# A looped TensorE stream, and a new path for x, in a one-token attention kernel that streams 554 MB

## The chip, the cores and the metric

The kernel runs on one core of one Trainium2 chip. The metric is the device time of one execution in microseconds (us).

Words used below: TensorE multiplies matrices, VectorE and ScalarE work on elements, SyncE's queue issues the large loads ("the main queue"), and ScalarE's queue is "the second queue". Each of the large loads is spread over 16 DMA engines (it leaves 16 completion records); it has landed when the last of the 16 has reported (in the kernel before, the 16 records of K31 came from 1230.87 to 1237.35 us, and the product that waits for it started at 1237.44 us). P.V is the product of the softmax weights with V. "K31" and "V31" are K and V of the last of the 32 heads, which are counted from 0. Engines get their instructions by DMA too: the profile lists these transfers as queues of kind "instruction" (q8 and q14). q8 carries TensorE's: 33 packets before. Such a transfer is called a fetch, and the 16 KB of one packet of q8 a block.

## The reference, cut to what matters

```python
# x: [1, 1, 640]   K, V caches: [1, 32 heads, 32768, 128]   all bf16
xn = layernorm(x)
q = (xn @ wq)                       # 32 heads of 128
p = softmax(q . k_cache * 128**-0.5)    # one query against 32768 keys, per head
out = x + (p . v_cache) @ wo + (silu(xn @ w_gate) * (xn @ w_up)) @ w_down
```

Each head needs 8.39 MB of K and 8.39 MB of V. With the weights that makes 554 MB, each byte read once.

## The kernel before

Three slots of 8.39 MB form a ring. The main queue loads wq, the feed-forward weights, then K0, K1, V0, K2, V1 and so on, at the end wo and the last V in five pieces. A load may start when its slot has been used up.

```python
@block.sync
def sp(e):
    e.dma_start(xb[:, :], A_x[0, 0:1, :].rearrange("o (p c) -> (o p) c", c=NCD)).then_inc(s_x, 16)  # 128 rows of 10 bytes
    for u in units:
        s = slot_of[u]
        if s in owner:
            e.wait_ge(*owner.pop(s))         # scores done (K slot) or P.V done (V slot)
        ...                                  # the load
```

VectorE multiplies K by the query in four pieces, TensorE sums each piece over groups of the head dimension with the identity as weights (`scores`), VectorE finishes the sums and the maximum, ScalarE takes the exponential. P.V of one head runs beside the next head's scores. TensorE's stream is one long straight line, written out for all 32 heads:

```python
@block.tensor
def pe(t):
    ...
    for k in range(NK):                      # 32 heads, written out
        scores(k)                            # 4 x 16 matmuls on the identity, 128x512 each
        ...
        total(h - 1)
        halves = pv_ops(h - 1, c); next(halves)   # 32 weight loads and 32 matmuls
        turn(h)                              # maximum over partitions
        next(halves)                         # 32 more
        spread(h)
        fold(h - 2)
    fold(H - 2)
    ...
    for h in range(H - 1): att(h)            # 155 one-column matmuls with wo
    total(H - 1)
    pv(H - 1, 0)                             # last head: 256 one-column matmuls, in five pieces as V lands
    att(H - 1)
```

Every wait is on a constant, for example `t.wait_ge(s_mul, n + 1)`.

## Time and profile before

| | before |
|---|---|
| time, median of 3 runs | 1299.28 us (1298.93 to 1299.52) |
| span of the profile | 1297.3 us |
| busy share: TensorE / VectorE / ScalarE | 80% / 52% / 4% |
| read from memory over the span | 427 GB/s |

From the page of the kernel before: the line of 40 slices (each digit is the busy share of the 16 DMA engines in tenths), the queue table (packets, MB, share of the 16 engines' span), and one group of TensorE's instructions (count, busy time and mean; then the idle time ahead of them and what ended most of it).

```profile
DMA  9999999999999999999999999999999999999997
...
q1 hardware_dynamic: 14848, 554.00, 99.2%
q8 instruction: 33, 0.54, 0.2%
q14 instruction: 6, 0.05, 0.0%
...
L245 PE MATMUL ps<-ring,ident 128*128 128x512 bf16 x128 | 56.2, 439 | 228.8 <-DVE ring L485 228.6
```

The DMA engines work from end to end: q1's packets alone take 99.2% of the 16 engines' span. The line L245 is the first score matmul of each piece: TensorE waits 228.6 us in all for VectorE there, so it is not what sets the pace. The queue's own timeline (start, duration, instruction) shows that it has a reserve too:

```profile
870.01 0.33 SPq L185 DMA_DIRECT2D ring<-in_A_v_cache_dram  x1
```

The load ahead of the one issued at 870.01 us lands on its fastest DMA engine at about 882 us, so the engines have 12 us of work left when a new load joins.

The same trace holds one record per DMA packet, and each transfer leaves 16 completion records. From them I computed, for eight loads, how far the last of the 16 lies behind the first. This is a computed table, not a view of the profile:

```
kernel before: time since wq's first packet (us) and spread of the 16 completions (us)
 load at    28   183   338   493   648   802   957  1112
 spread    1.2   1.9   1.9   3.4   3.4   4.9   4.9   6.4
```

The fastest engine takes 19.35 us per 8.39 MB load from first to last (8.39 MB / 19.35 us = 433.5 GB/s if all 16 went so), but others fall behind in steps of 1.5 us. The queue q8 suggests the reason: 33 instruction packets of 16,384 bytes, about one per head, 1.07 us each on average. The page counts 5142 matmuls and 3222 weight loads of TensorE, so a packet brings about 253 of its instructions (8364 / 33), and one instruction takes about 65 bytes. Every eight of them the spread grows by 1.5 us. At K31's landing seven of the 16 engines are within 1.6 us of the first, one is 4.3 us behind it, and eight are 4.8 to 6.5 us behind.

If all 16 engines kept the pace of the fastest, the load at 1112 us would land up to 6.4 us earlier (an estimate from the table). So the gain was sought with the slower engines; whether the fastest could go faster was not shown.

The end of the span, from the view by windows (us from the start; busy time of each engine, granted clock of TensorE, share of the DMA engines at work, GB/s):

```profile
core 0: us, PE busy (x) PEld busy (x) DVE busy (x) ACT busy (x) POOL busy (x), PEclk, DMA share, GB/s
...
1285.00:1288.00 3.00, 2.50 (x94) 2.41 (x91) 0.00 (x0) 0.00 (x0) 0.00 (x0) 0.50 0.58 236
1288.00:1290.00 2.00, 0.00 (x0) 0.00 (x0) 0.00 (x0) 0.00 (x0) 0.00 (x0) 0.50 0.44 172
```

Between 1285 and 1290 us only about half of the DMA engines still work: this is the spread again. And the timeline of the end (start, duration, engine, line, operation, count, idle time before and its releaser):

```profile
1237.44 17.43 DVE L485 TENSOR_TENSOR ring<-ring,qb 128x8192 bf16<-128x8192 bf16 x4 [2.85 <-DMA ring<-in_A_k_cache_dram]
...
1276.26 6.33 PE L340 MATMUL ps<-ocol,ring 128*128 128x1 bf16 x155 [0.36 <-ACT ocol L397]
...
1282.88 4.62 PE L270 MATMUL ps<-P,ring 128*128 128x1 bf16 x160
...
1290.12 2.72 PE L270 MATMUL ps<-P,ring 128*128 128x1 bf16 x96 [2.62 <-issue]
1292.87 0.22 DVE L514 TENSOR_SCALAR ocol<-ps,rzb 128x1 bf16<-128x1 f32 x1 [9.65 <-PE ps L270]
```

L485 is VectorE's product for the last head's K (K31), L340 the output product of heads 0 to 30, L270 the last head's P.V. There is a gap of 2.62 us in L270 after 160 of 256 columns, put down to "issue": a wait for nothing that the profile shows. (The last piece of V landed at 1290.41 us by its semaphore's records, the second piece, which holds columns 128 to 191, at 1285.51 us.) The start, for comparison with the change:

```profile
0.74 0.38 SPq L164 DMA_DIRECT2D xb<-in_A_x_dram  x1
...
1.18 0.41 SPq L171 DMA_DIRECT2D ring<-in_A_wq_dram  x1
...
52.42 8.76 DVE L485 TENSOR_TENSOR ring<-ring,qb 128x8192 bf16<-128x8192 bf16 x2 [6.30 <-DMA ring<-in_A_k_cache_dram]
```

### The profile page before, as it was taken

The numbers are of one execution on the slowest core, as the hardware profiler recorded it, in microseconds if no ns is written. First come the engines' busy times: TensorE is split into PE (matmuls) and PEld (weight loads), VectorE is DVE, ScalarE is ACT, GpSimd is POOL, SyncE is SP. The second block draws the span as 40 slices with busy tenths as digits, with TensorE's granted clock in tenths as the row PEclk, the third lists the DMA queues.
The fourth block names the chain that finished last, engine by engine and source line by source line (L and its number), as shares of the span: only waits on it lengthen the run. The fifth ranks groups of instructions, "written<-read, shape, count | busy, mean of one in ns | idle before, by whom it ended". The sixth has DMA issues, their size and how long they took to land.

```text
span 1297.3 us, 9428 instructions
## 1 busy us (share of the span) xinstructions
PE 1036.7 (80%) x5142; PEld 263.8 (20%) x3222; DVE 669.7 (52%) x406; ACT 50.8 (4%) x139; POOL 1.1 (0%) x8
## 2 busy tenths in 40 slices
PE   3678879877779877778877779877778978778977
PEld 1301222111222111222111222111222111222115
DVE  0485444666444666444666444666444566444560
ACT  2000000000000000000000000000000000000000
POOL 0000000000000000000000000000000000000000
PEclk9589889888889888889888889888889888889886
DMA  9999999999999999999999999999999999999997
GB/s 399 435 434 425 441 431 435 428 435 431 441 425 433 433 436 431 427 439 427 447 421 435 435 427 445 421 443 426 435 435 427 443 423 439 429 438 429 433 395 288
DMA packets 14887, 554.59 MB, mean 427 GB/s; under 512 B 1472, under 2 KB 5632, under 8 KB 5888
## 3 DMA queue, kind: packets, MB, share of 16 engines
q1 hardware_dynamic: 14848, 554.00, 99.2%
q8 instruction: 33, 0.54, 0.2%
q14 instruction: 6, 0.05, 0.0%
HBM read 553.99 MB, written 0.00 MB: 427 GB/s over the span
## 4 chain that ended last, share of the span: by engine, by line
DMA 52%; PE 30%; DVE 15%; issue 3%; SPq 0%; ACT 0%; DVEq 0%
DMA ring<-in_A_k_cache_dram 52%; PE ps L274 17%; DVE ring L485 14%; PE ps L228 10%; PE ps L245 1%; PE ps L270 1%; PE ps L340 1%; PE ps L310 0%; PE ps L304 0%; PE ps L295 0%; SPq L190 0%; DVE sc L493 0%; PE ps L316 0%; ACT o L392 0%; SPq L192 0%
## 5 line engine op out<-in xcount | busy, mean ns | idle before, releaser
L485 DVE TENSOR_TENSOR ring<-ring,qb 128x8192 bf16<-128x8192 bf16 x128 | 557.8, 4419 | 91.6 <-DMA ring<-in_A_k_cache_dram 91.6
L228 PE MATMUL ps<-ring,ident 128*128 128x512 bf16 x1920 | 495.3, 416 | 0.0
L274 PE MATMUL ps<-ring,P 128*4 128x512 bf16 x1984 | 438.3, 379 | 0.0
L245 PE MATMUL ps<-ring,ident 128*128 128x512 bf16 x128 | 56.2, 439 | 228.8 <-DVE ring L485 228.6
L274 PEld LDWEIGHTS ps<-ring,P 128*4 128x4 bf16 x1984 | 166.1, 85 | 245.3
L245 PEld LDWEIGHTS ps<-ring,ident 128*128 128x128 bf16 x128 | 12.6, 98 | 624.6 <-DVE ring L485 534.8
L508 DVE TENSOR_SCALAR negb<-ps 128x1 f32<-128x1 f32 x32 | 5.1, 158 | 215.5 <-PE ps L316 215.5
L493 DVE TENSOR_REDUCE sc<-ps 128x64 f32<-128x512 f32 x128 | 82.2, 683 | 62.1 <-PE ps L228 62.1
L503 DVE TENSOR_REDUCE m<-ps 1x1 f32<-1x128 f32 x32 | 8.9, 279 | 192.3 <-PE ps L310 192.3
L409 ACT ACTIVATE P<-sc,negb 128x256 bf16<-128x256 f32 x32 | 16.2, 508 | 1187.4 <-DVE negb L508 1187.4
L295 PE MATMUL ps<-identf,o 4*128 4x1 f32 x248 | 31.9, 245 | 0.9 <-ACT o L392 0.9
L304 PEld LDWEIGHTS ps<-rsum,ones 128*128 128x128 f32 x64 | 12.3, 194 | 99.2 <-issue 98.4
L295 PEld LDWEIGHTS ps<-identf,o 4*128 4x128 f32 x248 | 30.0, 187 | 0.9 <-ACT o L392 0.9
L392 ACT ACTIVATE o<-ps,rzb 4x512 f32<-4x512 f32 x31 | 21.0, 677 | 0.0
L220 PE MATMUL ps<-ring 128*128 128x512 bf16 x40 | 10.7, 436 | 11.7 <-DMA ring<-in_A_wq_dram 11.7
L454 DVE TENSOR_SCALAR sg<-sg 128x13 f32<-128x13 f32 (+1 forms) x2 | 0.2, 154 | 34.9 <-ACT sg L385 34.9
L500 DVE TENSOR_REDUCE pmax<-sc 128x1 f32<-128x256 f32 x32 | 13.4, 420 | 0.0
L310 PE MATMUL ps<-identf,pmax 128*1 128x128 f32 x64 | 12.2, 273 | 1.2 <-DVE pmax L500 1.2
L325 PE MATMUL ps<-xn,ring 128*128 128x1 bf16 (+1 forms) x140 | 8.7, 198 | 5.3 <-DMA ring<-in_B_w_down_dram 5.3
L316 PE MATMUL ps<-m,ones 1*128 1x1 f32 x64 | 12.1, 256 | 0.4 <-DVE m L503 0.4
L316 PEld LDWEIGHTS ps<-m,ones 1*128 1x128 f32 x64 | 9.4, 183 | 14.2 <-issue 13.5
L473 DVE RECIPROCAL rzb<-ps 128x1 f32<-128x1 f32 x32 | 5.0, 157 | 9.8 <-PE ps L304 9.8
(47 smaller groups left out, 87.8 us busy)
## 6 DMA issues: line engine op xcount, KB each, us to landing
ring<-in_A_wq_dram SPq DMA_DIRECT2D x1, 5120.0 KB, 15.3
ring<-in_A_wo_dram SPq DMA_DIRECT2D x1, 5120.0 KB, 36.7
ring<-in_A_v_cache_dram SPq DMA_DIRECT2D x1, 4096.0 KB, 22.0
ring<-in_B_w_gate_dram SPq DMA_DIRECT2D x1, 2160.0 KB, 20.0
ring<-in_B_w_up_dram SPq DMA_DIRECT2D x1, 2160.0 KB, 24.6
ring<-in_B_w_down_dram SPq DMA_DIRECT2D x1, 2080.0 KB, 28.6
ring<-in_A_v_cache_dram SPq DMA_DIRECT2D x1, 2048.0 KB, 21.4
ring<-in_A_v_cache_dram SPq DMA_DIRECT2D x1, 1024.0 KB, 23.3
```

Of the source, the lines that this page charges most:

```text
L228: return t.add_instruction(mybir.InstMatmult(start_tensor_calc=False, stop_tensor_calc=stop, tile_size=(128, 128), tile_position=(0, 0), l ...
L245: t.matmul(ob, lhsT=ident[:, :], rhs=src, start=True, stop=False)
L270: mm = t.matmul(OL, lhsT=ring[:, s, j * DH:(j + 1) * DH], rhs=P[:, h % PR, jj:jj + 1], start=(jj == 0), stop=(jj == NJ - 1))
L274: mm = t.matmul(O[h % 2], lhsT=P[:, h % PR, jj:jj + W], rhs=ring[:, s, j * DH:(j + W) * DH], start=(jj == 0), stop=(jj + W == NJ))
L295: mm = t.matmul(fold_ps, lhsT=o4[:, m * DH:(m + 1) * DH], rhs=identf[0:W, m:m + 1], start=(m == 0), stop=(m == W - 1))
L316: t.matmul(misc[:, 128:129], lhsT=ones[0:1, :], rhs=m1[0:1, h % SR:h % SR + 1], start=True, stop=True).then_inc(s_b, 1)
L340: mm = t.matmul(acc[:, c:c + 1], lhsT=wo_v[:, h, :, c], rhs=ocol[:, h:h + 1], start=(h == 0 and c == 0), stop=(h == H - 1), skip_group_che ...
L392: a.activation(out=o4[:, :], in_=O[h % 2], func=ACTF.Copy, scale=rzb[0:W, h % SR:h % SR + 1]).then_inc(s_o4, 1)
L409: a.activation(out=P[:, h % PR, :], in_=sc[:, h % SCR, :], func=ACTF.Exp, bias=negb[:, h % SR:h % SR + 1], scale=c_scale, accum_out=rsum[: ...
L485: v.tensor_tensor(out=kh, in0=kh, in1=q[:, None, :].to_broadcast([128, HF, DH]), op=ALU.mult).then_inc(s_mul, 1)
L493: v.tensor_reduce(out=sc[:, h % SCR, j:j + HF], in_=bank[n % NBK].rearrange("p (j e) -> p j e", e=G), axis=AX.X, op=ALU.add).then_inc(s_re ...
L500: v.tensor_reduce(out=pmax[:, h % SR:h % SR + 1], in_=sc[:, h % SCR, :], axis=AX.X, op=ALU.max).then_inc(s_max, 1)
```

## The change

There are two parts. TensorE's heads 2 to 31 become a loop of ten passes over three heads, so that TensorE's built program has 466 + 446 + 426 instructions (ahead of the loop, in it, behind it) in place of 5142, the separate weight loads not counted; what a wait counts to is then computed into a register. And x comes as one row on the second queue and is turned into a column by five small matmuls, so that wq is the first load of the main queue. To make three heads a period, the statistics slots go from 4 to 3 and the output bank from two to one; the wait for the feed-forward result moves ahead of the first head.

```diff
-    SR = 4
+    H0, PER = 2, 3
+    SR = 3
...
-            O = [ps8[0:W, 4, :], ps8[0:W, 5, :]]
+            O = ps8[0:W, 4, :]
...
             def sp(e):
-                e.dma_start(xb[:, :], A_x[0, 0:1, :].rearrange("o (p c) -> (o p) c", c=NCD)).then_inc(s_x, 16)
...
             def pe(t):
+                t.wait_ge(s_x, 16)
...
+                for c in range(NCD):
+                    mm = t.matmul(misc[:, 8 + c:9 + c], lhsT=xrow_v[:, :, c], rhs=one1[:, :], start=True, stop=True)
...
+                def wait(sem_of, h, count):
+                    n = count(h)
+                    if group[0] is not None:
+                        d = count(h + PER) - n
...
+                        n = group[0] * d + n          # a register
+                    t.wait_ge(sem_of, n)
...
-                for k in range(NK):
-                    scores(k)
-                    ...
+                for h in range(H0):
+                    head(h)
+                with t.Fori(0, (H - H0) // PER) as i:
+                    group[0] = i
+                    for h in range(H0, H0 + PER):
+                        head(h)
...
             def act(a):
+                a.dma_start(xrow, A_x[0, 0:1, :]).then_inc(s_x, 16)
```

More of the change, by code (lines that the diff above doesn't have):

```diff
@@ L33, in bass_parallel_sum__gqa_block_cached__swiglu_ffn__decode_kernel @@
     NJ = SK // 128
-    CH = NJ
-    NCH = NJ // CH
     HF = 64
-    NHF = CH // HF
-    NSTEP = NCH * NHF
+    NHF = NJ // HF
     G = 512 // HF
-    assert NJ % CH == 0 and CH % HF == 0 and DH % G == 0
-    CE = CH * DH
-    NK = H * NCH
+    assert NJ % HF == 0 and DH % G == 0
+    CE = NJ * DH
     FB = (F + 127) // 128
@@ L47, in bass_parallel_sum__gqa_block_cached__swiglu_ffn__decode_kernel @@
     SLOTS = 3
-    NBK = 4
-    SCR = 1
+    H0, PER = 2, 3
     PR = 3
-    SR = 4
+    SR = 3
     TAIL = [128, 64, 32, 16, 16]
     W = 512 // DH
-    assert sum(TAIL) == CH
+    assert sum(TAIL) == NJ and NHF == 4 and (H - H0) % PER == 0 and PER % SLOTS == 0
+    assert PER % PR == 0 and PER % SR == 0
     c_scale = float(DH) ** -0.5
@@ L60, in bass_parallel_sum__gqa_block_cached__swiglu_ffn__decode_kernel @@
     for h in range(H):
-        for c in range(NCH):
-            units.append(("k", h, c))
-            if h >= 1:
-                units.append(("v", h - 1, c))
-    units += [("wo",)]
-    units += [("v", H - 1, c) for c in range(NCH)]
+        units.append(("k", h))
+        if h >= 1:
+            units.append(("v", h - 1))
+    units += [("wo",), ("v", H - 1)]
     slot_of, use_of = {}, {}
@@ L75, in bass_parallel_sum__gqa_block_cached__swiglu_ffn__decode_kernel @@
     WQ_S, FFN_S, WO_S = slot_of[("wq",)], slot_of[("ffn",)], slot_of[("wo",)]
-    LASTV = ("v", H - 1, NCH - 1)
+    LASTV = ("v", H - 1)
     with ExitStack() as es:
@@ L86, in bass_parallel_sum__gqa_block_cached__swiglu_ffn__decode_kernel @@
         qb = sbt("qb", [128, H * DH], BF16)
-        sc = sbt("sc", [128, SCR, NJ], F32)
+        sc = sbt("sc", [128, NJ], F32)
         P = sbt("P", [128, PR, NJ], BF16)
@@ L95, in bass_parallel_sum__gqa_block_cached__swiglu_ffn__decode_kernel @@
         sg = sbt("sg", [128, 2, FB], F32)
-        xb = sbt("xb", [128, NCD], BF16)
+        one1 = sbt("one1", [1, 1], BF16)
         xf = sbt("xf", [128, NCD], F32)
@@ L129, in bass_parallel_sum__gqa_block_cached__swiglu_ffn__decode_kernel @@
         x0 = WQ_S * CE + NCD * H * DH
+        xrow = flat[0:1, x0 + NCD * 128:x0 + NCD * 128 + D]
+        xrow_v = xrow.rearrange("o (m c) -> o m c", c=NCD)
         xnb = flat[:, x0:x0 + NCD * 128].rearrange("p (c m) -> p c m", c=NCD)
-        assert NCD * (H * DH + 128) <= CE
+        assert NCD * (H * DH + 256) <= CE
         wq_v = wq.rearrange("p (c n) -> p c n", c=NCD)
@@ L155, in bass_parallel_sum__gqa_block_cached__swiglu_ffn__decode_kernel @@
             bank = [ps8[:, b, :] for b in range(8)]
-            O = [ps8[0:W, 4, :], ps8[0:W, 5, :]]
-            OL = ps8[:, 4 + (H - 1) % 2, 0:1]
+            O = ps8[0:W, 4, :]
+            OL = ps8[:, 5, 0:1]
             acc = ps8[:, 6, 0:NCD]
@@ L173, in sp @@
                     elif u[0] == "k":
-                        _, h, c = u
-                        e.dma_start(ring[:, s, :], kv_src(A_k_cache, h, c * CH, CH)).then_inc(s_slot[s], 16)
-                        owner[s] = (s_qk, NHF * (h * NCH + c + 1))
+                        e.dma_start(ring[:, s, :], kv_src(A_k_cache, u[1], 0, NJ)).then_inc(s_slot[s], 16)
+                        owner[s] = (s_qk, NHF * (u[1] + 1))
                     elif u == LASTV:
@@ L180, in sp @@
                             e.dma_start(ring[:, s, j * DH:(j + n) * DH],
-                                        kv_src(A_v_cache, H - 1, NJ - CH + j, n)).then_inc(s_tail[i], 16)
+                                        kv_src(A_v_cache, u[1], j, n)).then_inc(s_tail[i], 16)
                             j += n
                     elif u[0] == "v":
-                        _, h, c = u
-                        e.dma_start(ring[:, s, :], kv_src(A_v_cache, h, c * CH, CH)).then_inc(s_slot[s], 16)
-                        owner[s] = (s_pv, h * NCH + c + 1)
+                        e.dma_start(ring[:, s, :], kv_src(A_v_cache, u[1], 0, NJ)).then_inc(s_slot[s], 16)
+                        owner[s] = (s_pv, u[1] + 1)
                     elif u[0] == "ffn":
@@ L209, in pe @@
             def pe(t):
-                t.wait_ge(s_a, 3)
+                t.wait_ge(s_x, 16)
+                t.wait_ge(s_a, 2)
+                for c in range(NCD):
+                    mm = t.matmul(misc[:, 8 + c:9 + c], lhsT=xrow_v[:, :, c], rhs=one1[:, :], start=True, stop=True)
+                mm.then_inc(s_pa, 1)
+                t.wait_ge(s_a, 4)
                 t.matmul(misc[:, 0:1], lhsT=ones[:, :], rhs=st[:, 0:1], start=True, stop=True).then_inc(s_pa, 1)
-                t.wait_ge(s_a, 6)
+                t.wait_ge(s_a, 7)
                 t.matmul(misc[:, 1:2], lhsT=ones[:, :], rhs=st[:, 2:3], start=True, stop=True).then_inc(s_pa, 1)
-                t.wait_ge(s_a, 10)
+                t.wait_ge(s_a, 11)
                 t.wait_ge(s_wq, 16)
@@ L231, in again, with scores @@
                         ins=[nc.tensor.lower_ap(rhs), nc.tensor.lower_ap(lhsT)], outs=[nc.tensor.lower_ap(out)]))
-                def scores(k):
-                    h, c = divmod(k, NCH)
-                    kv = ring[:, slot_of[("k", h, c)], :].rearrange("p (j d) -> p j d", d=DH)
-                    for i in range(NHF):
-                        n = k * NHF + i
-                        t.wait_ge(s_mul, n + 1)
-                        if n >= NBK:
-                            t.wait_ge(s_red, n - NBK + 1)
-                        ob = bank[n % NBK].rearrange("p (j e) -> p j e", e=G)
+                group = [None]
+                def wait(sem_of, h, count):
+                    n = count(h)
+                    if group[0] is not None:
+                        d = count(h + PER) - n
+                        assert all(count(h + PER * i) == n + d * i for i in range((H - H0) // PER))
+                        n = group[0] * d + n
+                    t.wait_ge(sem_of, n)
+                def scores(h):
+                    kv = ring[:, slot_of[("k", h)], :].rearrange("p (j d) -> p j d", d=DH)
+                    for i in range(NHF):
+                        wait(s_mul, h, lambda h: NHF * h + i + 1)
+                        if h >= 1:
+                            wait(s_red, h, lambda h: NHF * (h - 1) + i + 1)
+                        ob = bank[i].rearrange("p (j e) -> p j e", e=G)
                         for g in range(DH // G):
@@ L248, in scores @@
                         mm.then_inc(s_qk, 1)
-                def pv_ops(h, c):
-                    u = ("v", h, c)
-                    s = slot_of[u]
-                    if c == 0:
-                        t.wait_ge(s_exp, h + 1)
-                        if h >= 2:
-                            t.wait_ge(s_o4, h - 1)
-                    parts = [(None, CH)]
-                    if u == LASTV:
-                        parts = list(enumerate(TAIL))
-                    j = 0
-                    for i, n in parts:
-                        if i is None:
-                            t.wait_ge(s_slot[s], 16 * use_of[u])
-                        else:
-                            t.wait_ge(s_tail[i], 16)
-                        end = j + n
-                        while j < end:
-                            jj = c * CH + j
-                            if h == H - 1:
-                                mm = t.matmul(OL, lhsT=ring[:, s, j * DH:(j + 1) * DH],
-                                              rhs=P[:, h % PR, jj:jj + 1], start=(jj == 0), stop=(jj == NJ - 1))
-                                j += 1
-                            else:
-                                mm = t.matmul(O[h % 2], lhsT=P[:, h % PR, jj:jj + W],
-                                              rhs=ring[:, s, j * DH:(j + W) * DH], start=(jj == 0),
-                                              stop=(jj + W == NJ))
-                                j += W
-                            if j == CH // 2:
-                                yield
@@ new lines, in pv_half @@
+                def pv_half(h, half):
+                    s = slot_of[("v", h)]
+                    if half == 0:
+                        wait(s_exp, h, lambda h: h + 1)
+                        wait(s_o4, h, lambda h: h)
+                        wait(s_slot[s], h, lambda h: 16 * use_of[("v", h)])
+                    for j in range(half * NJ // 2, (half + 1) * NJ // 2, W):
+                        mm = t.matmul(O, lhsT=P[:, h % PR, j:j + W], rhs=ring[:, s, j * DH:(j + W) * DH],
+                                      start=(j == 0), stop=(j + W == NJ))
+                    if half == 1:
+                        mm.then_inc(s_pv, 1)
@@ new lines, in pv_last @@
+                def pv_last():
+                    h = H - 1
+                    s = slot_of[LASTV]
+                    t.wait_ge(s_exp, H)
+                    j = 0
+                    for i, n in enumerate(TAIL):
+                        t.wait_ge(s_tail[i], 16)
+                        for _ in range(n):
+                            mm = t.matmul(OL, lhsT=ring[:, s, j * DH:(j + 1) * DH], rhs=P[:, h % PR, j:j + 1],
+                                          start=(j == 0), stop=(j == NJ - 1))
+                            j += 1
@@ L280, in pv_ops @@
                     mm.then_inc(s_pv, 1)
-                    yield
-                def pv(h, c):
-                    for _ in pv_ops(h, c):
-                        pass
                 def fold(h):
-                    t.wait_ge(s_o4, h + 1)
-                    if h == 0:
-                        t.wait_ge(s_fx, 1)
-                    else:
-                        t.wait_ge(s_ov, h)
+                    wait(s_o4, h, lambda h: h + 1)
+                    wait(s_ov, h, lambda h: h)
                     for m in range(W):
@@ L299, in total @@
                 def total(h):
-                    t.wait_ge(s_exp, h + 1)
-                    if h >= 1:
-                        t.wait_ge(s_rz, h)
+                    wait(s_exp, h, lambda h: h + 1)
+                    wait(s_rz, h, lambda h: h)
                     t.matmul(misc[:, 129:130], lhsT=ones[:, :], rhs=rsum[:, h % SR:h % SR + 1],
@@ L307, in turn @@
                 def turn(h):
-                    t.wait_ge(s_max, h + 1)
+                    wait(s_max, h, lambda h: h + 1)
                     t.matmul(misc[0:1, 0:128], lhsT=pmax[:, h % SR:h % SR + 1], rhs=identf[:, :],
@@ L313, in spread, with head @@
                 def spread(h):
-                    t.wait_ge(s_m, h + 1)
+                    wait(s_m, h, lambda h: h + 1)
                     t.matmul(misc[:, 128:129], lhsT=ones[0:1, :], rhs=m1[0:1, h % SR:h % SR + 1],
                              start=True, stop=True).then_inc(s_b, 1)
+                def head(h):
+                    scores(h)
+                    if h >= 1:
+                        total(h - 1)
+                        pv_half(h - 1, 0)
+                    turn(h)
+                    if h >= 1:
+                        pv_half(h - 1, 1)
+                    spread(h)
+                    if h >= 2:
+                        fold(h - 2)
                 t.wait_ge(s_ffn, 64)
@@ L342, in att @@
                     return mm
-                for k in range(NK):
-                    scores(k)
-                    h, c = divmod(k, NCH)
-                    if c < NCH - 1:
-                        if h >= 1:
-                            total(h - 1)
-                            pv(h - 1, c)
-                        continue
-                    if h >= 1:
-                        if NCH == 1:
-                            total(h - 1)
-                        halves = pv_ops(h - 1, c)
-                        next(halves)
-                    turn(h)
-                    if h >= 1:
-                        next(halves)
-                    spread(h)
-                    if h >= 2:
-                        fold(h - 2)
+                t.wait_ge(s_fx, 1)
+                for h in range(H0):
[4 more added lines that the diff above has]
+                        head(h)
+                    group[0] = None
                 fold(H - 2)
@@ L368, in pe @@
                 total(H - 1)
-                for c in range(NCH):
-                    pv(H - 1, c)
+                pv_last()
                 t.wait_ge(s_ov, H)
@@ L375, in act @@
             def act(a):
-                a.wait_ge(s_a, 7)
+                a.dma_start(xrow, A_x[0, 0:1, :]).then_inc(s_x, 16)
+                a.wait_ge(s_a, 8)
                 a.activation(out=st[:, 4:5], in_=st[:, 3:4], func=ACTF.Sqrt).then_inc(s_aa, 1)
@@ L388, in evac @@
                 def evac(h):
-                    a.wait_ge(s_pv, NCH * (h + 1))
+                    a.wait_ge(s_pv, h + 1)
                     a.wait_ge(s_rz, h + 1)
                     a.wait_ge(s_fold, h)
-                    a.activation(out=o4[:, :], in_=O[h % 2], func=ACTF.Copy,
+                    a.activation(out=o4[:, :], in_=O, func=ACTF.Copy,
                                  scale=rzb[0:W, h % SR:h % SR + 1]).then_inc(s_o4, 1)
@@ L405, in act @@
                     if h >= PR:
-                        a.wait_ge(s_pv, NCH * (h - PR + 1))
+                        a.wait_ge(s_pv, h - PR + 1)
                     if h >= SR:
                         a.wait_ge(s_z, h - SR + 1)
-                    a.activation(out=P[:, h % PR, :], in_=sc[:, h % SCR, :], func=ACTF.Exp,
+                    a.activation(out=P[:, h % PR, :], in_=sc[:, :], func=ACTF.Exp,
                                  bias=negb[:, h % SR:h % SR + 1], scale=c_scale,
@@ L425, in dve @@
                 step(v.memset(ones[:, :], 1.0))
-                v.wait_ge(s_x, 16)
-                step(v.tensor_copy(out=xf[:, :], in_=xb[:, :]))
+                step(v.memset(one1[:, :], 1.0))
+                v.wait_ge(s_pa, 1)
+                step(v.tensor_copy(out=xf[:, :], in_=misc[:, 8:8 + NCD]))
                 step(v.tensor_reduce(out=st[:, 0:1], in_=xf[:, :], axis=AX.X, op=ALU.add))
-                v.wait_ge(s_pa, 1)
+                v.wait_ge(s_pa, 2)
                 step(v.tensor_scalar(out=st[:, 1:2], in0=misc[:, 0:1], scalar1=1.0 / D, scalar2=None,
@@ L435, in dve @@
                                             op0=ALU.mult, op1=ALU.add, accum_out=st[:, 2:3]))
-                v.wait_ge(s_pa, 2)
+                v.wait_ge(s_pa, 3)
                 step(v.tensor_scalar(out=st[:, 3:4], in0=misc[:, 1:2], scalar1=1.0 / D, scalar2=eps,
@@ L443, in dve @@
                 step(v.tensor_copy(out=xnb[:, :, :], in_=xn[:, :, None].to_broadcast([128, NCD, 128])))
-                assert n_a[0] == 10
+                assert n_a[0] == 11
                 v.wait_ge(s_fa, 2)
@@ L473, in rz @@
                     v.reciprocal(out=rzb[:, h % SR:h % SR + 1], in_=misc[:, 129:130]).then_inc(s_rz, 1)
-                for k in range(NK):
-                    h, c = divmod(k, NCH)
-                    u = ("k", h, c)
+                for h in range(H):
+                    u = ("k", h)
                     s = slot_of[u]
@@ L486, in dve @@
                                         op=ALU.mult).then_inc(s_mul, 1)
-                    if c == 0 and h >= SCR:
-                        v.wait_ge(s_exp, h - SCR + 1)
+                    if h >= 1:
+                        v.wait_ge(s_exp, h)
                     for i in range(NHF):
-                        n = k * NHF + i
-                        v.wait_ge(s_qk, n + 1)
-                        j = c * CH + i * HF
-                        v.tensor_reduce(out=sc[:, h % SCR, j:j + HF],
-                                        in_=bank[n % NBK].rearrange("p (j e) -> p j e", e=G),
+                        v.wait_ge(s_qk, h * NHF + i + 1)
+                        v.tensor_reduce(out=sc[:, i * HF:(i + 1) * HF],
+                                        in_=bank[i].rearrange("p (j e) -> p j e", e=G),
@@ L495, in dve @@
                                         axis=AX.X, op=ALU.add).then_inc(s_red, 1)
-                    if c == 0 and h >= 1:
+                    if h >= 1:
                         rz(h - 1)
-                    if c == NCH - 1:
-                        v.wait_ge(s_red, NSTEP * (h + 1))
-                        v.tensor_reduce(out=pmax[:, h % SR:h % SR + 1], in_=sc[:, h % SCR, :],
-                                        axis=AX.X, op=ALU.max).then_inc(s_max, 1)
-                        v.wait_ge(s_t, h + 1)
-                        v.tensor_reduce(out=m1[0:1, h % SR:h % SR + 1], in_=misc[0:1, 0:128],
-                                        axis=AX.X, op=ALU.max).then_inc(s_m, 1)
-                        v.wait_ge(s_b, h + 1)
-                        if h >= SR:
-                            v.wait_ge(s_exp, h - SR + 1)
-                        v.tensor_scalar(out=negb[:, h % SR:h % SR + 1], in0=misc[:, 128:129], scalar1=-c_scale,
-                                        scalar2=None, op0=ALU.mult).then_inc(s_neg, 1)
+                    v.wait_ge(s_red, NHF * (h + 1))
@@ new lines, in dve @@
+                    v.tensor_reduce(out=pmax[:, h % SR:h % SR + 1], in_=sc[:, :],
+                                    axis=AX.X, op=ALU.max).then_inc(s_max, 1)
+                    v.wait_ge(s_t, h + 1)
+                    v.tensor_reduce(out=m1[0:1, h % SR:h % SR + 1], in_=misc[0:1, 0:128],
+                                    axis=AX.X, op=ALU.max).then_inc(s_m, 1)
+                    v.wait_ge(s_b, h + 1)
+                    if h >= SR:
+                        v.wait_ge(s_exp, h - SR + 1)
@@ L510, in dve @@
+                    v.tensor_scalar(out=negb[:, h % SR:h % SR + 1], in0=misc[:, 128:129], scalar1=-c_scale,
+                                    scalar2=None, op0=ALU.mult).then_inc(s_neg, 1)
                 rz(H - 1)
                 h = H - 1
-                v.wait_ge(s_pv, NCH * H)
+                v.wait_ge(s_pv, H)
                 v.wait_ge(s_rz, H)
```

## The prediction

> **What bounds it now.** The DMA engines. The slices show DMA 9 everywhere at 421–447 GB/s; the windows give a DMA share of 0.99–1.02 from 20 us to 1250 us. TensorE is 80% busy but not the limit: in the queue's own timeline each K or V load is issued 11–19 us before the loads ahead of it have drained (V issued at 870.0 us, the load ahead ends at 882), so TensorE may be later by about 11 us per head without starving the queue. It also waits for VectorE's product (waits: L245 on L485, up to 8.1 us).
>
> At 1285–1290 us only 0.58, then 0.44, of the DMA engines still work: they finish unevenly. The packet records of the trace say why: the 16 completions of one load spread over 1.9 us at 50 us, but over 6.5 us at 1240 us, and the spread grows in steps of about 1.5 us per instruction fetch (queue table: q8, 33 packets of 16 KB, one per head, 1.02–1.12 us each). Some eight engines are hit in turn, about four times each[...]. A load has landed when its last engine is done.
>
> **What the change does.**
> 1. TensorE's heads 2 to 31 become ten passes over three heads: some 710 instructions per pass (45 KB, three to four blocks). If these stay resident, fetches fall from 33 to about 8, the spread stays near 2–3 us, and K31, V31 and all behind them come about 4.5 us earlier (estimate: three fetches fewer on each hit engine, 1.5 us each). [...] If every back-branch refetches, there are 45–55 fetches: 2–3 more per hit engine, +3 to +5 us, or up to +10 us if the same engines are hit each time. I give residence 60%.
> 2. Back-branch and register waits: [...] lie within TensorE's wait and the queue's 11 us: about 0. Only the last head counts: TensorE has 2.6 us of slack before the last V piece at 1290.1 us. +0.3 us.
> 3. x leaves the main queue: its issue (0.38 us) goes, so wq is issued at 0.74 instead of 1.18 us: −0.4 us for the whole stream. x may be 1–3 us later; the normalised x is ready at 6.8 us and wq lands at 16.5 us: free.
> 4. One output bank instead of two, three statistics slots instead of four: the output copy (L392, 0.68 us) ends over 20 us before the next accumulation starts. Free.
>
> **Sum.** Resident: 1299.3 − 4.5 − 0.4 + 0.3 ≈ 1294.7. Refetching: about 1302 to 1308. Predicted 1295.5 us, 80% range 1292 to 1303. Faster by over 2%: 0.02; within: 0.96; slower: 0.02.
>
> **What would show it.** q8 packets: about 8 or less means resident, 45 or more refetching. Spread of K31's completions: 2–3 us against 6.5, and the DMA share near the end falls sharply instead of 0.58, 0.44. First K multiply (52.42 us before) starts about 0.4 us earlier. L485's wait for DMA and the 41.9 us K landing stay.
>
> **What would make it wrong.** Branch misses that hit one DMA engine repeatedly; a stall above 11 us per pass; the tail becoming TensorE's instead of DMA's.

The sum: 1299.3 − 4.5 − 0.4 + 0.3 ≈ 1294.7 us if a pass is resident, that is, not fetched again. The 60% for residence is the author's estimate; the "about 0" for branches and waits names room that was measured but no measured cost, and the +0.3 us for the tail is a guess without one. The 45 KB of a pass follow from the 65 bytes per instruction above, and the 45 to 55 fetches are an estimate: ten passes of three to four blocks, and the rest of the program.

## The result and the profile after

The changed kernel takes 1294.38 us (median of 4 runs, 1294.18 to 1294.48), against 1299.26 us (1298.93 to 1299.52) before. The ratio is 0.9962, with a 95% interval of 0.9945 to 0.998: clear of noise, and well under the 2% from which a change is called faster here. Ratios here are the mean time of one kernel's fast runs over that of the other's fast runs of the same rounds, so they are not quite the ratio of the medians that are quoted.

From the page after, the queue table and the group that answers to L245:

```profile
q8 instruction: 9, 0.15, 0.0%
q14 instruction: 6, 0.05, 0.0%
...
L254 PE MATMUL ps<-ring,ident 128*128 128x512 bf16 x128 | 56.1, 439 | 224.2 <-DVE ring L479 223.6
```

q8 has 9 packets in place of 33. TensorE still waits for VectorE for nearly as long (223.6 us against 228.6 us in that group), so whatever branches and register work cost fits into that wait. The computed table of the spread:

```
kernel after: time since wq's first packet (us), spread of the 16 completions, spread without the last one (us)
 load at       28   183   338   493   648   803   957  1112
 spread       1.1   1.9   1.8   2.1   2.0   3.0   3.0   4.0
 15 of 16     0.9   1.8   1.8   1.8   1.8   1.7   1.8   1.8
```

Fifteen engines stay together within 1.8 us. One falls behind, in steps of about 1.0 us; the steps come with the packets of q14 at 445, 755 and 1066 us (those at 127, 383 and 1199 us leave no step in the spread). The windows of the end:

```profile
core 0: us, PE busy (x) PEld busy (x) DVE busy (x) ACT busy (x) POOL busy (x), PEclk, DMA share, GB/s
...
1285.00:1288.00 3.00, 2.22 (x78) 2.08 (x76) 0.00 (x0) 0.00 (x0) 0.00 (x0) 0.50 0.08 29
1288.00:1290.00 2.00, 0.83 (x21) 0.67 (x20) 0.39 (x2) 0.00 (x0) 0.00 (x0) 0.50 0.00 0
```

The data are in by 1288 us, and the long half-busy stretch is gone. The timeline of the end:

```profile
1234.59 17.43 DVE L479 TENSOR_TENSOR ring<-ring,qb 128x8192 bf16<-128x8192 bf16 x4 [2.84 <-DMA ring<-in_A_k_cache_dram]
...
1280.02 1.76 PE L279 MATMUL ps<-P,ring 128*128 128x1 bf16 x61
...
1282.06 3.55 PE L279 MATMUL ps<-P,ring 128*128 128x1 bf16 x128 [0.27 <-issue]
...
1285.80 1.50 PE L279 MATMUL ps<-P,ring 128*128 128x1 bf16 x51 [0.19 <-issue]
...
1287.88 0.59 PE L279 MATMUL ps<-P,ring 128*128 128x1 bf16 x16 [0.59 <-DMA ring<-in_A_v_cache_dram]
1288.51 0.22 DVE L505 TENSOR_SCALAR ocol<-ps,rzb 128x1 bf16<-128x1 f32 x1 [8.14 <-PE ps L279]
```

K31's product (L479) starts at 1234.59 us, 2.85 us earlier. The last head's columns (L279) now run with gaps of 0.27 and 0.19 us and end on a wait for the last piece of V. The start:

```profile
0.73 0.51 ACTq L369 DMA_DIRECT2D ring<-in_A_x_dram  x1
...
0.74 0.39 SPq L166 DMA_DIRECT2D ring<-in_A_wq_dram  x1
...
51.95 8.76 DVE L479 TENSOR_TENSOR ring<-ring,qb 128x8192 bf16<-128x8192 bf16 x2 [6.39 <-DMA ring<-in_A_k_cache_dram]
```

wq is issued at 0.74 us in place of 1.18 us, and the first product of K starts 0.47 us earlier in these two profiles.

Taken from the two timelines and the semaphore records of the last load, the way to the last head's output goes like this:

```
                                   before     after   difference
K31's product starts              1237.44   1234.59     -2.85
last piece of V has landed        1290.41   1287.84     -2.57
last head's P.V ends              1292.84   1288.47     -4.37
```

So the time came mainly from two places: the stream lands 2.57 us earlier at its end, and TensorE finishes 0.63 us after the last landing in place of 2.43 us, which is another 1.80 us. Of the 4.90 us between these two profiled runs, 0.23 us more lie behind the last P.V and 0.30 us outside the span. Single profiles are good to a few tenths here: the same changed kernel, run again (after_again below), has K31's product at 1235.01 us.

### The profile page after: what moved, and what is told of

It reads as the page before. It is cut to its first block, busy times and chain, and to the rows that moved or that the text cites. A ratio compares the mean times of both kernels' runs of the same rounds, so it can differ in the third digit from the quotient of the medians.

```text
span 1292.7 us, 9645 instructions
## 1 busy us (share of the span) xinstructions
PE 1040.2 (80%) x5147; PEld 264.2 (20%) x3227; DVE 669.9 (52%) x407; ACT 50.8 (4%) x139; POOL 1.1 (0%) x8
## 4 chain that ended last, share of the span: by engine, by line
DMA 54%; PE 30%; DVE 13%; issue 2%; SPq 1%; DVEq 0%
DMA ring<-in_A_k_cache_dram 52%; PE ps L266 16%; DVE ring L479 13%; PE ps L227 12%; DMA ring<-in_A_v_cache_dram 2%; PE ps L254 1%; SPq L174 1%; PE ps L303 0%; PE ps L297 0%; SPq L183 0%; DVE sc L485 0%; PE ps L279 0%; SPq L185 0%; DVE pmax L491 0%; SPq L182 0%
## 5 line engine op out<-in xcount | busy, mean ns | idle before, releaser
L479 DVE TENSOR_TENSOR ring<-ring,qb 128x8192 bf16<-128x8192 bf16 x128 | 557.8, 4421 | 88.4 <-DMA ring<-in_A_k_cache_dram 88.4
L254 PE MATMUL ps<-ring,ident 128*128 128x512 bf16 x128 | 56.1, 439 | 224.2 <-DVE ring L479 223.6
```

Of the source, the lines that this page charges most:

```text
L254: t.matmul(ob, lhsT=ident[:, :], rhs=src, start=True, stop=False)
L479: v.tensor_tensor(out=kh, in0=kh, in1=q[:, None, :].to_broadcast([128, HF, DH]), op=ALU.mult).then_inc(s_mul, 1)
```

## The experiments

Three explanations stood against each other at the start. Theory F: instruction fetches delay single DMA engines, and the loop removes the fetches. Rival R: the loop's waits, the single bank or the three slots do it. Rival X: the earlier start of the stream does it. Each run is timed against the kernel before on the same chip. The first four runs of the table shared one chip, the next four another.

| run | us, median (range), runs | before, same rounds | ratio, 95% interval | q8 packets | K31's product starts |
|---|---|---|---|---|---|
| loop_only | 1295.46 (1295.22 to 1295.54), 5 | 1299.43 | 0.9970 [0.9957, 0.9984] | 9 | 1235.09 |
| x_only | 1298.18 (1297.75 to 1298.45), 5 | 1299.43 | 0.9991 [0.9977, 1.0004] | 33 | 1237.16 |
| per15 | 1298.85 (1298.21 to 1299.42), 5 | 1299.43 | 0.9998 [0.9984, 1.0011] | 36 | 1237.23 |
| before_dose | 1306.43 (1305.88 to 1306.70), 4 | 1299.43 | 1.0055 [1.0039, 1.0070] | 65 | 1243.85 |
| after_again | 1294.30 (1294.07 to 1294.92), 5 | 1299.38 | 0.9961 [0.9947, 0.9974] | 9 | 1235.01 |
| after_dose | 1295.39 (1295.10 to 1295.45), 5 | 1299.38 | 0.9969 [0.9955, 0.9983] | 14 | 1234.78 |
| before_pad | 1299.49 (1299.20 to 1299.96), 4 | 1299.38 | 1.0002 [0.9986, 1.0017] | 33 | 1237.54 |
| dve_loop | 1293.76 (1293.52 to 1294.01), 5 | 1299.38 | 0.9957 [0.9943, 0.9970] | 9 | 1232.70 |
| x_row_main | 1294.94 (1294.78 to 1295.20), 5 | 1299.30 | 0.9968 [0.9954, 0.9981] | 9 | 1235.07 |
| x_rows_second | 1295.08 (1294.47 to 1295.20), 5 | 1299.30 | 0.9967 [0.9953, 0.9980] | 9 | 1235.03 |

All runs gave correct results. Differences of less than 1 us between two changed kernels are read from their ranges of five runs, and called unsure where these touch or were taken on different chips.

### loop_only and x_only: the two parts alone

```diff
 # loop_only: the changed kernel, with
-                a.dma_start(xrow, A_x[0, 0:1, :]).then_inc(s_x, 16)
+                e.dma_start(xb[:, :], A_x[0, 0:1, :].rearrange("o (p c) -> (o p) c", c=NCD)).then_inc(s_x, 16)
 # and without the five turning matmuls; x_only: the kernel before with the opposite edit
```

> The change without its second part: TensorE's loop stays, x comes again as 128 short rows on the main queue. Theory F (the gain is fetches that no longer delay the DMA engines, x is worth its issue time only): 1294.8 us, about 0.45 us above the whole change; 9 fetch packets of 16 KB on q8; K31's first product at about 1235.0 us. Rival X (the earlier start of the stream is what pays): about 1297 us or more.

> The kernel before with x as one row on the second queue and nothing else. Theory F: 1298.8 us, about 0.45 us below the kernel before; 33 fetch packets as before; first K multiply at about 51.95 us instead of 52.42 us. Rival X: 1296 us or less.

The loop alone gives 1295.46 us, 4.0 us below the kernel before; x alone gives 1298.18 us, 1.25 us below it (the ranges do not meet, but the interval of the ratio reaches 1.0004). The loop is the larger part, which Rival X denies. But x seems to be worth over two and a half times what Theory F allowed for it (0.45 us), seen from either side: 1.25 us without the loop, and 1295.46 − 1294.30 = 1.16 us with it (here the two kernels ran on different chips, whose runs of the kernel before differ by 0.05 us in the median).

### per15: the same loop with fifteen heads in a pass

```diff
-    H0, PER = 2, 3
+    H0, PER = 2, 15
```

> The changed kernel with fifteen heads in a pass instead of three (two passes): the same waits on registers, one output bank, three statistics slots and x row, but a loop body of about 14 blocks of 16 KB[...]. Theory F: at least 33 fetch packets on q8, completions of K31 spread over 6 us or more, its first product at about 1237.0 us, time 1297 to 1299 us. Rival R (the gain comes from the loop's waits, the single bank or the slots, not from fetches): 1294.4 us, with the first product of K31 at 1234.6 us, whatever the count of fetches.

That a body of about 14 blocks would be fetched again was an assumption; the run tests it.

The line of q8 on its page, and K31's product in its timeline:

```profile
q8 instruction: 36, 0.59, 0.2%
```

```profile
1237.23 17.43 DVE L479 TENSOR_TENSOR ring<-ring,qb 128x8192 bf16<-128x8192 bf16 x4 [2.76 <-DMA ring<-in_A_k_cache_dram]
```

36 packets, and K31's product at 1237.23 us, as in the kernel before with x's new path (1237.16 us in x_only). The time, 1298.85 us, gives back all of the loop's gain, although waits in registers, the single bank and the three slots are all still there. Rival R falls.

### before_dose and after_dose: twice the instructions, with and without a loop

```diff
+                def tiny(n):
+                    for _ in range(n):
+                        t.matmul(bank[0][:, 0:1], lhsT=ident[:, :], rhs=ident[:, 0:1], start=True, stop=True)
 # before_dose: tiny(128) at the end of each head; after_dose: tiny(128) at the start of each head
```

The 128 one-column matmuls write to a bank that the next scores overwrite. With their weight loads they are 256 instructions, that is one fetch block of 16 KB (the 32 doses brought 65 − 33 = 32 packets more), and 3.4 us of TensorE in its wait for VectorE.

> The kernel before with 128 one-column matmuls more at the end of each head (256 instructions, one fetch block per head), about 5 us in which TensorE would wait for VectorE anyway. Theory F: about 65 fetch packets; each hit DMA engine delayed four more times by 1.5 us, so completions of K31 spread over 12 us and the time is 1305 us (1303 to 1308). Rival W (fetches are harmless, TensorE has slack for the added work): 1299 to 1300 us.

> The changed kernel with the same 128 one-column matmuls per head (256 instructions), here at the start of each head, 3.4 us in which TensorE waits for VectorE anyway. A pass is now 5.8 blocks of 16 KB (93 KB). Theory F[...]: still resident, 9 to 12 fetch packets, spread of K31 as in the changed kernel (4 us), 1294 to 1295.5 us, although the same added work made the kernel before about 7 us slower. Rival 2P[...]: over 60 packets, 1303 us or more. Rival W (the added work itself cost the 7 us): 1301 us with few packets.

That this body would not be fetched again was an assumption too; the limits named for it and for Rival 2P are cut. By Rival 2P it is fetched again in every pass: ten passes of 5.8 blocks make about 58 packets, and the rest of the program comes on top.

The kernel before with the dose, its q8, then K31's product, the dose behind the last head (L235) and the first columns of the last P.V (L274):

```profile
q8 instruction: 65, 1.06, 0.3%
```

```profile
1243.85 17.43 DVE L490 TENSOR_TENSOR ring<-ring,qb 128x8192 bf16<-128x8192 bf16 x4 [3.33 <-DMA ring<-in_A_k_cache_dram]
...
1280.34 3.39 PE L235 MATMUL ps<-ident 128*128 128x1 bf16 x128
...
1292.49 4.61 PE L274 MATMUL ps<-P,ring 128*128 128x1 bf16 x160
```

65 packets in place of 33, K31's product 6.41 us later, the time 7.0 us longer. Of this, 5.97 us come with the stream: the last piece of V lands at 1296.38 us in place of 1290.41 us. The other 1.2 us lie in the tail, where the dose behind the last head (3.39 us of matmuls at 1280.34 us) stands ahead of the last P.V and nothing hides it; after_dose, with the dose at the start of each head, has no such piece. The spread grows twice as fast, again 1.5 us per eight fetches:

```
kernel before with twice the fetches
 load at    28   183   338   493   648   803   957  1112
 spread    1.3   1.9   3.5   5.0   6.6   8.1   9.6  11.2
```

The same number of added matmuls per head in the looped kernel, its q8, K31's product and the last head's columns (L283):

```profile
q8 instruction: 14, 0.23, 0.1%
```

```profile
1234.78 17.43 DVE L484 TENSOR_TENSOR ring<-ring,qb 128x8192 bf16<-128x8192 bf16 x4 [2.66 <-DMA ring<-in_A_k_cache_dram]
...
1280.21 1.76 PE L283 MATMUL ps<-P,ring 128*128 128x1 bf16 x61
...
1282.49 3.55 PE L283 MATMUL ps<-P,ring 128*128 128x1 bf16 x128 [0.52 <-issue]
...
1287.88 1.93 PE L283 MATMUL ps<-P,ring 128*128 128x1 bf16 x67 [1.84 <-issue]
```

14 packets: five more blocks of program, each fetched once. K31's product is not later than in the changed kernel beside it (1235.01 us in after_again). So the 6 us that the stream lost in before_dose were not the matmuls' own work, and the pass of about 1480 instructions (5.8 blocks, 93 KB; counted from the recorded instructions of a head) was not fetched again in its ten passes: q8 has no packet between 221 us and 1280 us. The 1.1 us that the time did grow come from the end: a gap of 1.84 us in the columns, of the kind that the next run explains. Rival 2P falls, and Rival W for all but the tail.

### before_pad: what the gap in the last head's columns is

```diff
+                tiny(48)           # once, ahead of the feed-forward stage, where TensorE waits for weights
                 t.wait_ge(s_ffn, 64)
```

> The kernel before with 48 one-column matmuls (96 instructions) ahead of the feed-forward stage, where TensorE waits for weights, so that every later fetch-block boundary falls 48 last-head columns earlier. Theory F says that the 2.6 us gap among the last head's columns (after column 160 of 256, no piece boundary of the data) is TensorE waiting for its own next block: the gap moves to about column 112 of 256, or goes if the block arrives in time. Rival D (it waits for a piece of V): the gap stays at column 160. Time 1297 to 1300 us.

The last head's columns in its timeline (L274):

```profile
1283.14 3.12 PE L274 MATMUL ps<-P,ring 128*128 128x1 bf16 x112
...
1288.56 3.57 PE L274 MATMUL ps<-P,ring 128*128 128x1 bf16 x128 [2.30 <-issue]
...
1292.57 0.59 PE L274 MATMUL ps<-P,ring 128*128 128x1 bf16 x16 [0.43 <-issue]
```

The gap of the kernel before was after column 160; it is now after column 112, where 96 instructions more, at two per column, put it. Boundaries of V's pieces lie at 128, 192, 224 and 240 and did not move; the first piece, with columns 0 to 127, had landed at 1280.96 us, 5 us ahead of the gap. A second, small gap comes 128 columns, or 256 instructions, later. So TensorE was waiting for its own next block, 2.62 us before and 2.30 us here, in a stretch where it uses up a block in 3.6 us. The time is the same (1299.49 us): moving the boundary does not remove it. Rival D falls. The packet records show the wait directly: q8's packet ended at 1288.72 us in the kernel before and at 1287.10 us here, and TensorE went on 1.40 and 1.46 us later. At all 18 such boundaries in the kept traces where a gap shows, long or short, it went on 1.3 to 1.5 us after the packet's end.

### after_again and dve_loop: the one engine that still lags

```diff
 # dve_loop: the changed kernel, with VectorE's heads 5 to 31 as nine passes over three heads
# (its wait for the whole query moves ahead of the first head)
+                    q = qb[:, bass.ds(vgroup[0] * (PER * DH) + h * DH, DH)]
...
+                with v.Fori(0, (H - V0) // PER) as vi:
+                    vgroup[0] = vi
+                    for h in range(V0, V0 + PER):
+                        vhead(h)
```

> The changed kernel itself once more, so that the runs beside it can be compared with it on one chip. 1294.4 us, 9 fetch packets of 16 KB, completions of K31 spread over 4.0 us with a single engine beyond 1.8 us.

> The changed kernel with VectorE's stream as a loop over three heads too (from head 5 on, query taken at an address in a register). The one DMA engine that still lags in the changed kernel (4.0 us at K31, the next 1.8 us) is put down to VectorE's own 8 KB fetches on q14. Theory F: q14 shows 2 fetches inside the stream instead of 6, the spread of K31 falls to 2 us, its first product comes 2 us earlier (about 1232.7 us) and the time falls by 0.5 to 2 us to about 1293 us. Rival S (that engine is slow for another reason): spread 4 us as before, 1294.4 us or a little more for the register work.

The changed kernel repeats: 1294.30 us, spread of K31 4.4 us with the next engine at 2.0 us. With VectorE looped, the instruction queues on the page, then K31's product and the last head's columns in the timeline:

```profile
q8 instruction: 9, 0.15, 0.0%
q14 instruction: 3, 0.02, 0.0%
```

```profile
1232.70 17.43 DVE L491 TENSOR_TENSOR ring<-ring,qb 128x8192 bf16<-128x8192 bf16 x4 [2.75 <-DMA ring<-in_A_k_cache_dram]
...
1278.14 1.77 PE L279 MATMUL ps<-P,ring 128*128 128x1 bf16 x61
...
1280.27 3.55 PE L279 MATMUL ps<-P,ring 128*128 128x1 bf16 x128 [0.37 <-issue]
...
1286.21 1.93 PE L279 MATMUL ps<-P,ring 128*128 128x1 bf16 x67 [2.38 <-issue]
```

q14 falls from 6 packets to 3 (2 were expected; the three that are gone are those at 445, 755 and 1066 us), the spread of K31 from 4.4 to 1.9 us, and K31's product starts 2.31 us earlier than in after_again. That engine's lag was VectorE's own fetching; Rival S falls. The time falls by only 0.54 us, to 1293.76 us, with ranges that just do not meet (0.06 us apart). The rest went into the gap that before_pad explained: the last piece of V lands 2.31 us earlier (1285.96 us, against 1288.27 us in after_again), but TensorE waits 2.38 us for its next block after column 189. dve_loop is the fastest version, by a little.

### x_row_main and x_rows_second: which half of x's new path pays

```diff
 # x_row_main: the changed kernel, with x's row issued first on the main queue
-                a.dma_start(xrow, A_x[0, 0:1, :]).then_inc(s_x, 16)
+                e.dma_start(xrow, A_x[0, 0:1, :]).then_inc(s_x, 16)
 # x_rows_second: loop_only, with the 128 short rows issued on the second queue instead
```

> The changed kernel with x still as one row, but issued first on the main queue. With x on the second queue the whole x part was worth about 1.1 us (1295.46 without it, 1294.3 with it), not the 0.44 us of its issue time. If the gain is the freed issue ahead of wq: about 1294.8 us or more, first K multiply near 52.5 us. If it is the shape (one row in place of 128 short ones): 1294.3 us.

> The changed kernel with x as 128 short rows, as before, but issued on the second queue, without the five turning matmuls. If the gain is the freed issue ahead of wq: 1294.3 us, first K multiply near 52.15 us. If it is the shape: about 1295.4 us.

Both expectations were either-or, and neither came out alone. The row on the main queue gives 1294.94 us, the rows on the second queue 1295.08 us; both lie between 1294.30 us (both halves) and 1295.46 us (neither). The ranges of both touch that of the changed kernel (up to 1294.92 us), so how much either half gives is unsure. The second queue does start the stream earlier: the first K product is at 52.13 us with rows on it and at 52.45 us with the row on the main queue. With x on the second queue, the part of the time that lies outside the profile's span is shorter too: its medians are 1.55 to 1.69 us in the six kernels of the table that have x there, and 1.78 to 1.91 us in the others and the kernel before. Whether one row in place of 128 saves anything by itself is left open; no run looked inside that.

## Why the prediction was right, and where it was not

The range and the point held: 1295.5 us predicted, 1294.38 us measured. The range, 1292 to 1303 us, includes the time of the kernel before, so that it held says little. The residence that it gave 60% is what happened (q8 has no packet between 220 and 1279 us), and its sum for that case was 1294.7 us. The mechanism, fetches that delay DMA engines, passed per15, both dose runs and dve_loop. That the sum came within 0.3 us is luck: the stream gave 2.57 us where 4.9 us were forecast, the tail gave 1.80 us where it was to cost 0.3 us, and these two errors cancel. Term by term:

- **Residence.** "fetches fall from 33 to about 8": 9. Right.
- **"K31, V31 and all behind them come about 4.5 us earlier", and the "spread stays near 2–3 us".** Mis-sized. K31's product came 2.85 us earlier, x's share included, and the spread was 4.0 us. TensorE's fetches did go, and 15 engines stayed within 1.8 us. The prediction did not look at q14, three of whose packets held one engine back by about 1.0 us each; with VectorE looped too, the spread was 1.9 us and K31's product came 1237.44 − 1232.70 = 4.74 us earlier, x's share included.
- **"Only the last head counts: TensorE has 2.6 us of slack before the last V piece at 1290.1 us. +0.3 us."** Wrong in kind. The 2.6 us gap was no slack but TensorE waiting for its own instructions, as before_pad showed. With smaller gaps in the changed kernel, TensorE ended 0.63 us after the last landing in place of 2.43 us: −1.8 us, not +0.3 us. This nearly made up for the previous point. The gaps are small after the change (0.2 to 0.3 us) because the block's packet came sooner: it began 1.40 us after TensorE had entered the block before (at 1282.06 us), but 3.74 us after it in the kernel before, 3.01 us in after_dose (gap 1.84 us) and 3.41 us in dve_loop (gap 2.38 us). What decides when the packet begins is not shown.
- **x: "−0.4 us for the whole stream".** The stream starts 0.3 to 0.5 us earlier, as predicted, but the part is worth 1.1 to 1.25 us in time. Of the rest, 0.2 to 0.35 us lie outside the span; about half of the whole is not explained. That the later x costs nothing was right: normalised x is ready at 6.94 us after the change and at 6.82 us before, and wq lands at about 16 us.
- **Branch, register waits, one bank, three slots: "about 0".** Right as far as the runs go: per15 has all of them and lies 0.67 us above x_only, with three fetches more and its last piece of V 1.63 us later (1291.76 us against 1290.13 us); that rest was not followed up.

## What to carry to other kernels

When every DMA engine is busy from end to end, look at the engines one by one: a load has landed only with its last share (K31's last record came 6.5 us after its first), and instruction fetches of a long straight program are transfers like others: here each of TensorE's (16 KB) held one engine back by about 1.5 us, on eight of the 16 in turn, and three of VectorE's (8 KB) held one back by about 1.0 us each, as far as the spread of the completions shows (the records do not name the engine). A loop pays here not by doing less work but because its body was not fetched again (9 packets in place of 33; 14 with a pass of 5.8 blocks); with a body of about 14 blocks, which was fetched again (per15, 36 packets), its gain was gone. Where between these two sizes the limit lies was not measured. And a gap marked as a wait for nothing visible (2.62 us here) should be suspected of being a wait for instructions before it is counted as slack; shifting the program by a known number of instructions tells.
